# Attention and gated experts in one kernel: late attention steps between whole expert chunks, a reordered fifth pair, weight merges in two steps, two bank copies of seven on DVE

## The chip, the cores and the metric

The kernel runs on one core of one Trainium2 chip. The metric is the device time of one execution in microseconds; what is shown is the median of several runs. A profile is one further execution, with its own time.

## The reference

The program first does attention over 8 batches x 8 heads, 576 positions and 64 columns a head, with a mask by blocks of 64, and then passes the heads' outputs, 4608 tokens of 512 columns, through a two-layer feed-forward with a sigmoid gate.

```
scores = scale * np.matmul(q, k.transpose(0, 1, 3, 2))       # scale = 1/8
scores = np.where(block_i >= block_j, scores, -1e9)          # blocks of 64
attn = np.exp(scores - scores.max(-1, keepdims=True))
attn = attn / (attn.sum(-1, keepdims=True) + 1e-9)
x = np.matmul(attn, v).transpose(0, 2, 1, 3).reshape(B * S, H * D)
h = x @ w_in                                                 # 512 -> 2048
out = (h * (1 / (1 + np.exp(-1.702 * h)))) @ w_out           # 2048 -> 512
```

The weights arrive as 64-bit floats, and the kernel makes 32-bit floats of them itself.

## The kernel before, in words

**Attention.** Two heads make a pair; there are 32 pairs, four to a batch, and "the first pair" is pair 0. A pair's 576 queries go in five chunks, 0 to 4, of growing width (chunk i sees the keys up to its own blocks). `score` makes the scores of a list of chunks on TensorE (PE) into PSUM banks, DVE adds the mask and takes the row's extreme (`weigh`, L351), ACT takes the exponential (L358), DVE makes the reciprocal of the sum (L368, L371), and POOL, or DVE for chunk 4 of the late pairs, scales (`normalise`, L376, L378). The result must be transposed before the sum over the values. In the first eight pairs ("early") PE does it (`flip`, L102) and ACT copies the banks to SBUF (L411; the narrow tails L424). In the later pairs DVE transposes 32x32 blocks (`turn`, L385 the wide part, L390 the narrow one) and 16 DMAs move the blocks. `av` is the sum over the values on PE; ACT copies its bank to the ring `xr` (L450, L451). `prep` transposes the next pair's q and k on DVE (L297) and starts the load of the pair after.

**Order of the attention steps.** Three strings in `ORDER` give the steps of a pair in slots, one string for each phase (pairs 0 to 3, 4 to 7, 8 and later); `START` stands for pair 4 and `HANDOVER` for pair 8. Digits are chunks to score ("3+0/2+1": two banks for 3 and 0, two for 2 and 1), V is `av` of the pair before, L is `prep` of the next pair, a, B and C are flips (a: chunks 0 and 1 of this pair; B: 2 and 3 of the one before; C: 4 of the one before), and a dash is an empty slot. After each slot the main loop lets weights be converted up to a quota (`WEIGHTS_BY`: position, pieces; a pair is two positions) and experts run up to a quota (`TILES_BY`).

**Experts.** `moe` is a generator. Tokens go in 12 tiles of 384, the hidden columns in 16 chunks of 128. Numbers are split into a high and a low part (`split` for the tokens: xh on ACT, L498, xl on DVE, L82), and each product is three matmuls. A chunk is 12 matmuls into the bank `hp`, then ACT's tanh (L555), DVE's `g` (L556), ACT's `gh` (L564) and POOL's `gl` (L82); behind the 12 matmuls `second` issues the nine of the chunk before into three `acc` banks. There is one `hp` bank. The generator yields after every three matmuls, and `advance` stops there as soon as the quota is reached, so an attention step can stand within the 12 or within the nine.

**Weights.** There are 32 pieces of 128x512. `begin` has ACT scale the word that holds the exponent, to a PSUM bank (L219); `merge` puts the 32-bit word together on DVE in three steps (L223 shift, L229 sign, L234 low bits); `split_weights` makes the high part on ACT (L243) and the low part on POOL (L82). Each piece uses the same bank, and the merged word `z` stands in one of two rooms by turns for the first 28 pieces. The first tile's chunks call `convert` themselves for what they need.

Within an engine the instructions stand in one order; a scheduler makes it from the order of the code and from priorities (`tc.high_priority`), and PE's matmuls keep the order of the code.

Of the kernel before, what the change touches and what calls it, by code (L numbers as in the profile page):

```python
# [13 lines left out]
AF = mybir.ActivationFunctionType  # L14
ALU = mybir.AluOpType
# [10 lines left out]
ORDER = (  # L26
# [3 lines left out]
)  # L30

START = "1+0 - B 2/3 L C - V - 4 - a - - -"
HANDOVER = "B C - 3+0/2+1 - - V - - - 4 - - L - -"


WEIGHTS_BY = ((0, 0), (8, 13), (14.5, 32))
TILES_BY = ((8.4, 0), (17, 1), (33.7, 4), (65.7, -2))


# [1 line left out]
def attention_moe_kernel(  # L41
# [9 lines left out]
    nc = tc.nc  # L51
# [19 lines left out]
    def f(ap):  # L71
        return ap.bitcast(F32)
# [141 lines left out]

    def begin(j):

        bits[j] = ps.tile([P, 512], F32, tag="w3", name="wm")
        for w, c in parts[j]:
            nc.scalar.activation(out=bits[j][:, c], in_=f(w[..., 1]), func=AF.Copy, scale=2.0**-112)  # L219

    def merge(j):
        u = bits.pop(j).bitcast(U32)
        nc.vector.tensor_scalar(  # L223
            out=u, in0=u, scalar1=3, scalar2=None, op0=ALU.logical_shift_left
        )

        z = whole[j] = room("e1" if j % 2 and j < 2 * len(places) else "wm", [P, WC], U32, "wm")
        for w, c in parts[j]:
            nc.vector.scalar_tensor_tensor(  # L229
                out=u[:, c], in0=w[..., 1], scalar=0x80000000, in1=u[:, c],  # L230
                op0=ALU.bitwise_and, op1=ALU.bitwise_or,
            )
        for w, c in parts.pop(j):
            nc.vector.scalar_tensor_tensor(  # L234
                out=z[:, c], in0=w[..., 0], scalar=29, in1=u[:, c],
                op0=ALU.logical_shift_right, op1=ALU.bitwise_or,
            )

    def split_weights(j):
# [52 lines left out]
    def prep(n):  # L292

        tag = "e0" if early(n) and n % 2 else "qk"
        qk[n] = d2.tile([P, 2, S], F32, tag=tag, name="qk", bufs=1)
        for x in range(2):
            nc.vector.transpose(out=qk[n][:, x], in_=raw[n][:, x].rearrange("p c d -> p (c d)"))  # L297
        raw.pop(n)
        m = follower(n)
        if m is not None:  # L300
            load(m)
# [99 lines left out]
    def flip(n, chunks):  # L401

        for i in chunks:
            todo = [(j, hd) for j in range(i) for hd in range(2)]
            for x in range(0, len(todo), 4):
                part = todo[x : x + 4]
                bk = bank()
                for y, (j, hd) in enumerate(part):
                    tr(out=bk[:, y * P : (y + 1) * P], in_=es[i][:, hd, j * P : (j + 1) * P], identity=ident)
                s0 = SLOT[i] + part[0][0]  # L410
                nc.scalar.copy(  # L411
                    out=pw[:, :, s0 : s0 + len(part) // 2].rearrange("p b s h c -> p (s h) b c"),
                    in_=bk[:, 0 : len(part) * P].rearrange("p (x b c) -> p x b c", b=4, c=32),
                )

        bk = bank()
        todo = [(i, hd) for i in chunks for hd in range(2)]
        for y, (i, hd) in enumerate(todo):
            tr(out=bk[0:BLK, y * P : (y + 1) * P], in_=es[i][:, hd, i * P : width(i)], identity=ident)
        src = bk[0:BLK, 0 : len(todo) * P].rearrange("p (x b c) -> p x b c", b=4, c=32)  # L420
        for part in ([0], [1]) if 0 in chunks else (chunks,):
            i, x, a = part[0], 2 * chunks.index(part[0]), 2 if part[0] else 0
            s0 = 9 + max(i, 1)
            nc.scalar.copy(  # L424
                out=pw[0:BLK, a : a + 2, s0 : s0 + len(part)].rearrange("p b s h c -> p (s h) b c"),
                in_=src[:, x : x + 2 * len(part), a : a + 2],
            )
# [81 lines left out]
    def moe():  # L509
# [17 lines left out]
        for t in range(NT):  # L527
            tt = TILES[t][1]
            if t == 0:
                yield ("tile", 0)  # L530
                split(0)
            xh, xl = xs["xh"], xs["xl"]
            acc = [ps.tile([P, DM], F32, tag=f"acc{c}", name=f"acc{c}") for c in range(tt // P)]
            for fc in range(NFC):
                if t == 0:
                    convert(fc // FG * GROUP + NDC + fc % FG + 1)
                hp = ps.tile([P, 512], F32, tag="h", name="hp")
                fs = slice(fc % FG * P, (fc % FG + 1) * P)
# [12 lines left out]
                gh = d2.tile([P, TT], F32R, tag="gh", name="gh")[:, 0:tt]  # L551
                gl = d2.tile([P, TT], F32R, tag="gl", name="gl")[:, 0:tt]

                with tc.high_priority(offset=300):
                    nc.scalar.activation(out=g, in_=hp[:, 0:tt], func=AF.Tanh, scale=1.702)  # L555
                    nc.vector.scalar_tensor_tensor(  # L556
                        out=g, in0=g, scalar=1.0, in1=hp[:, 0:tt], op0=ALU.add, op1=ALU.mult
                    )

                if fc == NFC - 1 and t + 1 < NT:  # L560
                    yield ("tile", t + 1)
                    split(t + 1)
                with tc.high_priority(offset=300):
                    nc.scalar.copy(out=gh, in_=g)  # L564
                    subtract(nc.gpsimd, gl, g, f(gh))
                if prev is not None:
                    yield from second(prev)
                prev = (gh, gl, fc, acc, t)
        yield from second(prev)


# [7 lines left out]
        return -(-sum(TILES[t]) // S) * H  # L579

    mo = moe()
    state = {"t": 0.0, "wait": None, "done": False}

    def advance(heads_done, until):
        while not state["done"] and not until():
            if state["wait"] is not None:
                if heads_for(state["wait"]) > heads_done:
                    return
# [2 lines left out]
            if got is None:  # L591
                state["done"] = True
            elif isinstance(got, tuple):
                state["wait"] = got[1]
            else:
                state["t"] += got

    def before_av(n):
# [53 lines left out]
```

## Time and profile before

| | |
|---|---|
| median of 3 runs | 1127.14 us (1125.93 to 1127.29) |
| the profiled execution, its own time | 1124.21 us |
| its span, first to last instruction | 1122.4 us |
| mean granted TensorE clock | 0.989 |
| busy: PE, DVE, ACT, POOL | 1076.8, 585.3, 497.9, 407.2 us |
| read from and written to HBM | 45.09 and 9.44 MB |

The page has the engines' busy time, the same in 40 slices, and the costliest groups of instructions by line, with the idle time of the engine ahead of them and what ended it. A row of the timeline gives start, duration, engine, line, operation, out<-in and shapes, and in brackets the idle time ahead and its releaser. Consecutive matmuls overlap in these rows, so their pace is the distance of their starts.

### The profile page before, as it was taken

The page shows a single profiled execution, that of the slowest core. Times are in us where ns is not written, and L with a number is a line of the kernel's source. Part 1 is how long each engine was busy: PE and PEld are TensorE (multiplying, and loading weights), DVE is VectorE, ACT ScalarE, POOL GpSimd, SP SyncE. Part 2 cuts the span into 40 slices and gives each one's busy share as a digit, 9 for nine tenths or more (in the row PEclk, how much of TensorE's full clock was granted, in tenths as well). Part 3 has the DMA queues.
Part 4 walks back from the last instruction along what each step waited for, and adds up shares of the span by engine and source line. Part 5 has one row for each costly group of instructions (what it writes and reads, how often), then busy time and mean ns, then how long its engine had stood idle before and what let it go on. Part 6 is the DMA issues. An engine that isn't in the chain of part 4 may idle for free. (4 is left out here: it accounts for less than half of the span.)

```text
span 1122.4 us, 20015 instructions
## 1 busy us (share of the span) xinstructions
PE 1076.8 (96%) x6960; PEld 910.8 (81%) x6960; DVE 585.3 (52%) x1856; ACT 497.9 (44%) x1321; POOL 407.2 (36%) x509
## 2 busy tenths in 40 slices
PE   5979998999999999999999999999999999999998
PEld 3757776788788888888888888888888888999997
DVE  6785885555555645655545655654545655111210
ACT  5865776434434534433443543443434444322322
POOL 4665674333333333233333333333333233222222
PEclk8979999999999999999999999999999999999999
DMA  8734533233443433243443333244343331200000
GB/s 167 207 89 153 144 69 72 77 80 64 103 86 79 102 88 72 56 109 64 95 100 79 81 94 68 52 113 86 74 111 73 70 87 46 54 29 1 29 1 29
DMA packets 219366, 91.26 MB, mean 81 GB/s; under 512 B 197760, under 2 KB 197760, under 8 KB 219264
## 3 DMA queue, kind: packets, MB, share of 16 engines
q1 hardware_dynamic: 214528, 89.38, 33.9%
q8 instruction: 55, 0.90, 0.3%
q10 hardware_dynamic: 4736, 0.59, 0.3%
q14 instruction: 47, 0.39, 0.1%
HBM read 45.09 MB, written 9.44 MB: 49 GB/s over the span
## 5 line engine op out<-in xcount | busy, mean ns | idle before, releaser
L82 POOL TENSOR_TENSOR gl<-g,gh 128x384 fp32r<-128x384 f32 x192 | 194.8, 1015 | 538.8 <-ACT gh L564 448.1
L99 PE MATMUL hp<-xh,wih 128*128 128x384 f32 x768 | 265.2, 345 | 11.7 <-DVE g L556 10.9
L556 DVE SCALAR_TENSOR_TENSOR g<-g,hp 128x384 f32<-128x384 f32 x192 | 105.5, 550 | 326.4 <-ACT g L555 325.4
L99 PE MATMUL hp<-xh,wil 128*128 128x384 f32 x768 | 259.3, 338 | 0.1
L99 PE MATMUL hp<-xl,wih 128*128 128x384 f32 x768 | 254.5, 338 | 0.6 <-DVE xl L82 0.4
L555 ACT ACTIVATE g<-hp 128x384 f32<-128x384 f32 x192 | 94.1, 490 | 339.9 <-PE hp L99 337.7
L99 PE MATMUL acc<-woh,gh 128*128 128x512 f32 x576 | 232.1, 403 | 0.0
L99 PE MATMUL acc<-woh,gl 128*128 128x512 f32 x576 | 227.2, 394 | 0.5 <-POOL gl L82 0.5
L99 PE MATMUL acc<-wol,gh 128*128 128x512 f32 x576 | 227.6, 395 | 0.0
L99 PEld LDWEIGHTS hp<-xh,wih 128*128 128x128 f32 x768 | 144.5, 188 | 36.4 <-DVE g L556 21.8
L564 ACT CAST gh<-g 128x384 fp32r<-128x384 f32 x192 | 98.5, 513 | 147.9 <-DVE g L556 147.8
L358 ACT ACTIVATE e<-e,mx 64x64 f32<-64x64 f32 (+4 forms) x240 | 132.4, 552 | 63.6 <-DVE mx L351 63.6
L376 POOL TENSOR_TENSOR e<-e,sm 64x64 f32<-64x64 f32 (+1 forms) x192 | 114.1, 614 | 108.9 <-DVE sm L371 62.0
L99 PEld LDWEIGHTS hp<-xh,wil 128*128 128x128 f32 x768 | 144.7, 188 | 7.4 <-POOL wil L82 0.7
L99 PEld LDWEIGHTS hp<-xl,wih 128*128 128x128 f32 x768 | 144.1, 188 | 1.7 <-DVE xl L82 1.7
L99 PE MATMUL bank<-qk 64*128 64x320 f32 (+4 forms) x768 | 122.2, 428 | 14.2 <-DVE qk L297 11.1
L99 PEld LDWEIGHTS acc<-woh,gh 128*128 128x128 f32 x576 | 108.3, 188 | 30.6 <-issue 10.7
L99 PEld LDWEIGHTS acc<-wol,gh 128*128 128x128 f32 x576 | 108.1, 188 | 23.5 <-POOL wol L82 0.2
L99 PEld LDWEIGHTS acc<-woh,gl 128*128 128x128 f32 x576 | 108.3, 188 | 16.8 <-POOL gl L82 1.2
L385 DVE STREAM_TRANSPOSE turned<-e 128x384 f32<-128x384 f32 (+1 forms) x192 | 92.4, 499 | 48.2 <-POOL e L376 48.2
L99 PEld LDWEIGHTS bank<-qk 64*128 64x128 f32 x768 | 69.8, 194 | 56.5 <-issue 26.5
L351 DVE CUSTOM_DVE_ANT_0 e<-bank,mask 64x64 f32<-64x64 f32 (+4 forms) x240 | 88.3, 417 | 29.8 <-PE bank L99 26.4
(50 smaller groups left out, 960.5 us busy)
## 6 DMA issues: line engine op xcount, KB each, us to landing
turned<-turned SPq DMA_DIRECT2D x192, 80.0 KB, 2.1
turned<-turned SPq DMA_DIRECT2D x96, 112.0 KB, 2.2
raw<-in_q_dram SPq DMA_DIRECT2D x128, 72.0 KB, 2.5
out_dram<-osb SPq DMA_DIRECT2D x36, 256.0 KB, 2.2
raw<-in_k_dram SPq DMA_DIRECT2D x120, 72.0 KB, 2.5
turned<-turned SPq DMA_DIRECT2D x96, 88.0 KB, 2.1
words<-in_moe_w_in_dram SPq DMA_DIRECT2D x16, 512.0 KB, 6.1
vp<-in_v_dram SPq DMA_DIRECT2D x60, 128.0 KB, 2.3
```

Source lines behind the costliest of these rows:

```text
L82: eng.tensor_tensor(out=out, in0=in0, in1=in1, op=ALU.subtract)
L99: return tc.keep_in_program_order(nc.tensor.matmul(**kw))
L351: nc.vector.tensor_tensor_reduce(out=e[0:m, hd, lo:hi], in0=s, in1=mk, op0=ALU.add, op1=ALU.min, scale=-0.125, scalar=3e38 if lo == 0 else ...
L358: nc.scalar.activation(out=e[0:m, hd], in_=e[0:m, hd], func=AF.Exp, scale=-1.0, bias=mx[0:m, i, hd : hd + 1], accum_out=sm[0:m, i, hd : hd ...
L376: nc.gpsimd.tensor_tensor(out=x, in0=x, in1=sc.to_broadcast([m, width(i)]), op=ALU.mult)
L385: nc.vector.transpose(out=tw[:, :, SLOT[i] : SLOT[i] + i, hd].rearrange("p b j c -> p j b c"), in_=e[:, hd, 0 : i * P],)
L555: nc.scalar.activation(out=g, in_=hp[:, 0:tt], func=AF.Tanh, scale=1.702)
L556: nc.vector.scalar_tensor_tensor(out=g, in0=g, scalar=1.0, in1=hp[:, 0:tt], op0=ALU.add, op1=ALU.mult)
L564: nc.scalar.copy(out=gh, in_=g)
```

## The change

1. `advance` goes on, from pair 9 on, until the generator stands at an "edge": behind the nine matmuls of a chunk and ahead of the next chunk's 12. In those pairs an attention step no longer stands within a chunk.
2. In the late pairs' string and at the hand-over V stands one slot earlier or nearer the scores; at the hand-over C stands one slot later.
3. `START`: in the fifth pair B comes first, and C and V of the fourth pair stand ahead of the fifth's scores 2 and 3.
4. The merge has two DVE steps: first z = low word >> 29, then z = (bank << 3) | z. The sign now comes with ACT's pass, which is Prelu with a slope of -2^32 where it was Copy.
5. Of a pair's seven wide bank copies in `flip`, DVE takes two: the first bank of chunk 3 and the first of chunk 4.
6. `WEIGHTS_BY` asks for 11 pieces by position 6.5, none more until 8.9, and all 32 by 14.5.
7. The transposes of `prep` get a higher priority up to pair 4.

```
-    "3+0/2+1 - - - - V - 4 - - - L -",
+    "3+0/2+1 - - - V - - 4 - - - L -",
-START = "1+0 - B 2/3 L C - V - 4 - a - - -"
-HANDOVER = "B C - 3+0/2+1 - - V - - - 4 - - L - -"
-WEIGHTS_BY = ((0, 0), (8, 13), (14.5, 32))
+START = "B 1+0 C V - L 2/3 - - 4 - a - -"
+HANDOVER = "B - C - 3+0/2+1 - - V - - 4 - - L - -"
+WEIGHTS_BY = ((0, 0), (6.5, 11), (8.9, 11), (14.5, 32))
...
-            nc.scalar.activation(out=bits[j][:, c], in_=f(w[..., 1]), func=AF.Copy, scale=2.0**-112)
+            nc.scalar.activation(
+                out=bits[j][:, c], in_=f(w[..., 1]), func=AF.Prelu, scale=2.0**-112, alpha=-(2.0**32)
+            )
...
-        nc.vector.tensor_scalar(
-            out=u, in0=u, scalar1=3, scalar2=None, op0=ALU.logical_shift_left
-        )
-        for w, c in parts[j]:
+        for w, c in parts.pop(j):
+            nc.vector.tensor_scalar(
+                out=z[:, c], in0=w[..., 0], scalar1=29, scalar2=None, op0=ALU.logical_shift_right
+            )
             nc.vector.scalar_tensor_tensor(
-                out=u[:, c], in0=w[..., 1], scalar=0x80000000, in1=u[:, c],
-                op0=ALU.bitwise_and, op1=ALU.bitwise_or,
-            )
-        for w, c in parts.pop(j):
-            nc.vector.scalar_tensor_tensor(
-                out=z[:, c], in0=w[..., 0], scalar=29, in1=u[:, c],
-                op0=ALU.logical_shift_right, op1=ALU.bitwise_or,
+                out=z[:, c], in0=u[:, c], scalar=3, in1=z[:, c],
+                op0=ALU.logical_shift_left, op1=ALU.bitwise_or,
             )
...
+        with tc.high_priority(offset=300 if n <= HP else 0):
+            for x in range(2):
+                nc.vector.transpose(out=qk[n][:, x], in_=raw[n][:, x].rearrange("p c d -> p (c d)"))
...
-                nc.scalar.copy(
+                (nc.vector.tensor_copy if i > 2 and x == 0 else nc.scalar.copy)(
...
                 prev = (gh, gl, fc, acc, t)
+                yield ("edge", fc)
...
-        while not state["done"] and not until():
+        while not state["done"] and not (until() and (state["edge"] or turns["n"] <= 2 * HP)):
...
             elif isinstance(got, tuple):
-                state["wait"] = got[1]
+                if got[0] == "tile":
+                    state["wait"] = got[1]
+                else:
+                    state["edge"] = True
             else:
+                state["edge"] = False
                 state["t"] += got
```

How this moves instructions is seen in the order in which each engine's instructions stand. PE, at the first group of scores of a late pair; bank<-qk are scores, hp and acc are the experts. Before:

```order
L99 MATMUL hp<-xh,wil 128x384
L99 MATMUL hp<-xl,wih 128x384
L99 MATMUL bank<-qk 128x448 x2
L99 MATMUL bank<-qk 128x64 x2
L99 MATMUL bank<-qk 128x320 x2
L99 MATMUL bank<-qk 128x192 x2
L99 MATMUL acc_5869<-woh,gh 128x512
L99 MATMUL acc_5869<-woh,gl 128x512
```

and now:

```order
L99 MATMUL acc_5839<-woh,gl 128x512
L99 MATMUL acc_5839<-wol,gh 128x512
L99 MATMUL bank<-qk 128x448 x2
L99 MATMUL bank<-qk 128x64 x2
L99 MATMUL bank<-qk 128x320 x2
L99 MATMUL bank<-qk 128x192 x2
L99 MATMUL hp<-xh,wih 128x384
L99 MATMUL hp<-xh,wil 128x384
```

The scores stood between a chunk's 12 and the nine of the one before; now they stand ahead of a chunk's 12.

DVE, from the first scores of a late pair on, in the changed program; it reads alike in many pairs before, and in other pairs of both the first g stands ahead of the second narrow transpose (L389 here, L390 before; L384 is the wide one, g<-g,hp is the step that frees hp):

```order
L367 TENSOR_SCALAR sm<-sm 64x2
L370 RECIPROCAL sm<-sm 64x2
L389 STREAM_TRANSPOSE turned<-e 64x2x2x32
L367 TENSOR_SCALAR sm<-sm 128x2
L370 RECIPROCAL sm<-sm 128x2
L389 STREAM_TRANSPOSE turned<-e 64x2x2x32
L556 SCALAR_TENSOR_TENSOR g<-g,hp 128x384 x2
L384 STREAM_TRANSPOSE turned<-e 128x3x4x32 x2
```

DVE did not move here, but the first g now belongs to the chunk right behind the scores.

DVE, behind the scores of chunk 4 of a late pair. Before:

```order
L368 TENSOR_SCALAR sm<-sm 128x2
L371 RECIPROCAL sm<-sm 128x2
L378 TENSOR_SCALAR e<-e,sm 128x576 x2
L385 STREAM_TRANSPOSE turned<-e 128x4x4x32 x2
L556 SCALAR_TENSOR_TENSOR g<-g,hp 128x384
L390 STREAM_TRANSPOSE turned<-e 64x2x2x32
```

and now:

```order
L367 TENSOR_SCALAR sm<-sm 128x2
L370 RECIPROCAL sm<-sm 128x2
L377 TENSOR_SCALAR e<-e,sm 128x576 x2
L556 SCALAR_TENSOR_TENSOR g<-g,hp 128x384
L384 STREAM_TRANSPOSE turned<-e 128x4x4x32 x2
L389 STREAM_TRANSPOSE turned<-e 64x2x2x32
```

The g moved ahead of the two wide transposes; in some pairs it stands between the two scalings.

ACT, up to the copy of the fourth pair's V (xr<-bank 128x512). Before:

```order
L243 CAST woh<-wm 128x512
L219 ACTIVATE wm<-words 128x512
L358 ACTIVATE turned,sm<-turned,mx 128x320 x2
L358 ACTIVATE turned,sm<-turned,mx 128x448 x2
L411 COPY turned<-bank 128x4x4x32
L243 CAST wih<-wm 128x512
L219 ACTIVATE wm<-words 128x512
L411 COPY turned<-bank 128x4x4x32
L424 COPY turned<-bank 64x2x2x32
L451 COPY xr<-bank 128x512
```

and now:

```order
L241 CAST wih<-wm 128x512
L220 ACTIVATE wm<-words 128x512
L411 COPY turned<-bank 128x4x4x32
L424 COPY turned<-bank 64x2x2x32
L241 CAST wih<-wm 128x512
L220 ACTIVATE wm<-words 128x512
L450 COPY xr<-bank 128x64
L451 COPY xr<-bank 128x512
```

The exponentials of the fifth pair's chunks 2 and 3 (320 and 448 wide) left the stretch, and one wide bank copy went to DVE.

More of the change, by code (lines that the diff above doesn't have):

```diff
@@ L295, in prep @@
         qk[n] = d2.tile([P, 2, S], F32, tag=tag, name="qk", bufs=1)
-        for x in range(2):
-            nc.vector.transpose(out=qk[n][:, x], in_=raw[n][:, x].rearrange("p c d -> p (c d)"))
+        with tc.high_priority(offset=300 if n <= HP else 0):
+            for x in range(2):
+                nc.vector.transpose(out=qk[n][:, x], in_=raw[n][:, x].rearrange("p c d -> p (c d)"))
         raw.pop(n)
@@ L581, in attention_moe_kernel @@
     mo = moe()
-    state = {"t": 0.0, "wait": None, "done": False}
+    state = {"t": 0.0, "wait": None, "done": False, "edge": True}
     def advance(heads_done, until):
-        while not state["done"] and not until():
+        while not state["done"] and not (until() and (state["edge"] or turns["n"] <= 2 * HP)):
             if state["wait"] is not None:
```

## The prediction

> **What bounds the kernel now.** I read the page first, then the busy time by stretches, then the waits and the timeline at the places that the change touches. The page:
>
> ```profile
> span 1122.4 us, 20015 instructions
> PE 1076.8 (96%) x6960; PEld 910.8 (81%) x6960; DVE 585.3 (52%) x1856; ACT 497.9 (44%) x1321; POOL 407.2 (36%) x509
> PEclk8979999999999999999999999999999999999999
> ```
>
> TensorE is busy for 96% of the span, so only time in which it waits can be won. The stretches (span, then busy time of PE, PEld, DVE, ACT, POOL, granted clock) say where it waits:
>
> ```profile
> 0.00:90.00 90.00, 67.37 (x515) 49.79 (x516) 66.15 (x217) 60.16 (x176) 51.22 (x74) 0.87 0.60 144
> 90.00:215.00 125.00, 115.12 (x793) 92.44 (x793) 87.06 (x252) 82.59 (x216) 69.11 (x76) 1.00 0.40 107
> 215.00:985.00 770.00, 760.84 (x4992) 648.58 (x4991) 412.44 (x1354) 316.87 (x854) 254.38 (x327) 1.00 0.36 81
> 985.00:1110.00 125.00, 125.00 (x629) 113.37 (x628) 18.52 (x34) 34.59 (x70) 30.51 (x30) 1.00 0.04 13
> ```
>
> PE idles 22.6 us in the first 90, 9.9 in the next 125, 9.2 in the 770 of the late pairs, and nothing in the pure expert stretch. The change works on the first three. What the last one shows is the floor of a chunk, from the chain of waits:
>
> ```profile
> 1003.03 2.10 PE hp L99 x12
> 1005.14 2.08 PE acc L99 x9
> ```
>
> A chunk costs 4.18 us, and everything below is measured against it.
>
> **Late pairs: the wait that goes, and the one that comes.** The waits between 230 and 985 us have one line for PE's long waits, and the timeline shows one of them (PE, then DVE):
>
> ```profile
> PE hp L99 <- DVE g L556: 9.2, 21, 1.6
> ...
> 629.56 0.40 PE L99 MATMUL acc<-wol,gh 128*128 128x512 f32 x1
> 630.19 0.44 PE L99 MATMUL hp<-xh,wih 128*128 128x384 f32 x1 [0.23 <-DVE g L556]
> 630.47 0.34 PE L99 MATMUL hp<-xh,wil 128*128 128x384 f32 x1
> ...
> 627.53 0.95 DVE L378 TENSOR_SCALAR e<-e,sm 128x576 f32<-128x576 f32 x2
> 628.40 1.30 DVE L385 STREAM_TRANSPOSE turned<-e 128x512 f32<-128x512 f32 x2
> 629.62 0.51 DVE L556 SCALAR_TENSOR_TENSOR g<-g,hp 128x384 f32<-128x384 f32 x1
> ```
>
> There is one bank for hp, so a chunk can't begin before DVE has read the last one's hp in g (L556); here g stands behind two scalings and two transposes of chunk 4. The start distance is 0.63 instead of 2.08/9 = 0.23, so 0.40 are lost, of which the view counts 0.23 as idle; the matmul behind it follows after 0.28 instead of 2.10/12 = 0.175, another 0.11. So the 21 waits cost 9.2 + 21 x (0.17 + 0.11) = 15.1 us.
>
> With the change DVE's order puts g ahead of the two transposes (1.30 us). But attention now stands directly ahead of an hp, so a new wait is possible at two places. The rows for both (PE, DVE of the first group 3+0/2+1; PE, DVE of chunk 4):
>
> ```profile
> 604.37 2.11 PE L99 MATMUL bank<-qk 64*128 64x448 f32 x16
> 606.41 0.50 PE L99 MATMUL acc<-woh,gh 128*128 128x512 f32 x1
> ...
> 610.54 0.31 DVE L390 STREAM_TRANSPOSE turned<-e 64x128 f32<-64x128 f32 x1 [1.66 <-POOL e L376]
> ...
> 622.94 1.24 PE L99 MATMUL bank<-qk 64*128 64x256 f32 x8
> 624.11 0.49 PE L99 MATMUL acc<-woh,gh 128*128 128x512 f32 x1
> ...
> 623.66 0.55 DVE L556 SCALAR_TENSOR_TENSOR g<-g,hp 128x384 f32<-128x384 f32 x1
> 624.13 0.42 DVE L351 CUSTOM_DVE_ANT_0 e<-bank,mask 128x256 f32<-128x256 f32 x1
> ```
>
> *Behind 3+0/2+1.* The scores begin at U = 604.37; the next matmul is 2.04 later. In the new order that is hp, then acc, and the second hp is due at 2.04 + 0.11 + 2.10 + 2.08 = U + 6.33. Where DVE's g stands behind the last narrow transpose of chunk 3, which waits for POOL until U + 6.17, g ends at 6.17 + 0.31 + 0.55 = U + 7.03: 0.7 to 0.8 late, with the restart 0.9. Counted in the changed order, 12 of the 23 late pairs have it so; in the others g stands ahead of that transpose, or V stands between and pushes the hp back. 12 x 0.9 = 10.8 us.
>
> *Behind chunk 4.* Scores at T = 622.94, hp at T + 1.17, the second hp due at 1.17 + 0.11 + 4.18 = T + 5.46. DVE's scalings end at 628.48 = T + 5.54, after a reduction that began at T + 1.19 only because g (623.66) was ahead of it; the new g is done before. If the chain starts up to 0.46 sooner, g ends near T + 5.6, otherwise T + 6.05. That is 0.15 to 0.6 late; I take the near end, 0.3 with the restart, since that g is no longer in front. In 14 pairs g stands behind both scalings: 4.2 us. In the others it stands between them and is in time. Two pairs have the next tile's split ahead of this g; I give them a wait like today's, 0.5 each: 1.0.
>
> Sum: 10.8 + 4.2 + 1.0 = 16.0 against 15.1: **1 us lost**, so the late part nearly cancels. Bounds: 11 us won (the first wait absent), 10 lost (it stands in all 23 pairs: 11 more x 0.9). Behind a waiting hp stand the rest of its chunk and all later work of PE, so each wait counts in full. V one slot earlier costs nothing: it comes at least four chunks (17 us) after the scores of chunk 4, and the transposes that it needs end at 629.70, T + 6.8. The quotas still give six chunks a pair, and each interruption costs PE its two switches as before.
>
> **Start: to the first expert chunk.** ACT copies, DVE merges, the weights' ping-pong and V of the fourth pair (ACT; then PE; then groups):
>
> ```profile
> 58.13 0.62 ACT L243 CAST woh<-wm 128x512 fp32r<-128x512 f32 x1 [1.81 <-DVE wm L234]
> 61.57 0.62 ACT L243 CAST woh<-wm 128x512 fp32r<-128x512 f32 x1 [2.29 <-DVE wm L234]
> 65.00 0.62 ACT L243 CAST woh<-wm 128x512 fp32r<-128x512 f32 x1 [0.98 <-DVE wm L234]
> 70.50 0.57 ACT L358 ACTIVATE turned<-turned,mx 128x320 f32<-128x320 f32 x1
> ...
> 72.24 0.67 ACT L358 ACTIVATE turned<-turned,mx 128x448 f32<-128x448 f32 x1
> ...
> 75.96 0.58 ACT L451 COPY xr<-bank 128x512 f32<-128x512 f32 x1 [0.74 <-PE bank L99]
> ...
> 34.74 1.98 PE L99 MATMUL bank<-qk 64*128 64x320 f32 x8
> ...
> 76.71 0.44 PE L99 MATMUL hp<-xh,wih 128*128 128x384 f32 x1 [0.71 <-ACT xr L450]
> ...
> 81.83 0.45 PE L99 MATMUL hp<-xh,wih 128*128 128x384 f32 x1 [1.79 <-DVE g L556]
> ...
> L223 DVE TENSOR_SCALAR wm<-wm 128x512 uint32<-128x512 uint32 x32 | 22.3, 696 | 16.0 <-ACT wm L219 15.9
> L411 ACT COPY turned<-bank 128x512 f32<-128x512 f32 x32 | 17.4, 582 | 5.2 <-PE bank L102 5.0
> L82 POOL TENSOR_TENSOR wil<-wm,wih 128x512 fp32r<-128x512 f32 x16 | 20.5, 1280 | 14.1 <-ACT wih L243 13.0 <-PE hp L99 1.1
> ```
>
> A piece of weights turns over in 61.57 - 58.13 = 3.44 us, with ACT waiting for three DVE steps of 0.70. Two steps remain, and the first no longer needs ACT, so one step lies between ACT's two: about 1.4 less a piece. Of the 1.81 + 2.29 + 0.98 = 5.1 us of ACT idle, 1.5 stay: 3.6 won. Four bank copies of 0.58 leave ACT's queue in these two pairs: 2.3. The exponentials of the fifth pair's 2 and 3 (70.50 to 72.91) move behind V: 2.4. Two more pieces are converted ahead of V, as WEIGHTS_BY now asks: two ACT steps of 0.62 each, 2.5 lost. Their loads move ahead with them on SP's queue, two pieces before they are used: nothing. The four copies of the first two pairs give at most 2.3, half taken: 1.2. So V's copy at 75.96 comes 3.6 + 2.3 + 2.4 - 2.5 + 1.2 = 7.0 earlier; PE still has to do the moved scores (1.98): **5 us won** (0 to 8). Prelu for Copy is the same kind of ACT pass, and the new program has one table load as before: nothing. The fifth pair's transposes with a higher priority stand ahead of merges that they stood among: nothing, since V is not behind them. The first chunk then waits from 76.71 to 81.83 for 2.1 us of work; g is behind a conversion that is behind four xl on DVE. Three of them now stand ahead: **1 won** (0 to 2).
>
> The new first step reads SBUF and writes SBUF; no row has it. DVE and POOL side by side are seen in xl:
>
> ```profile
> 76.05 3.50 DVE L82 TENSOR_TENSOR xl<-xr,xh 128x384 fp32r<-128x384 f32 x4
> ...
> 192.41 1.51 DVE L82 TENSOR_TENSOR xl<-xr,xh 128x384 fp32r<-128x384 f32 x3 [7.24 <-ACT xh L498]
> ```
>
> 0.87 each while POOL works, 0.50 while it idles. So I take the new step no cheaper than the 0.70 of a removed one; 0.87 / 0.50 times that is its upper end, 0.5 us a piece, 1.5 over three. The Trainium skill (VectorE: DVE Perf Modes, "The perf-mode tier table") gives a 32-bit single-source step within SBUF twice the speed; by that it takes an estimated 0.35 and the sum would be 1 us better. The same skill (GPSIMD Engine Reference, the row "SBUF interfaces") has DVE instructions in such modes, or with two SBUF inputs, contend with GpSimd, and the two rows of xl agree.
>
> The clock was 0.87 over these 90 us; PE's matmuls at half clock are part of the losses. The Trainium skill (TensorE: Matmul & The Clock Gate, Part 1) ties half clock to an idle window of about 3.4 us; by it a start that idles 7 us less gets back an estimated 0.13 x 7 = 0.9 us more.
>
> **Fifth to eighth pair.** Over eight pairs DVE loses 32 steps of 0.70 (22 us) and gains 16 copies at 0.58 to 0.70, ACT's price and its own for 512 columns from a bank (9 to 11 us). Most of that lies beside PE's work; the hp waits for g that it can shorten are few: **1 won** (2 lost to 3 won). At the hand-over:
>
> ```profile
> 187.83 0.33 PE L102 MATMUL bank<-ident,turned 128*128 128x128 f32 x1 [1.07 <-POOL turned L376]
> 190.16 1.20 PE L102 MATMUL bank<-ident,turned 128*128 128x128 f32 x9 [2.00 <-POOL turned L376]
> ```
>
> PE waits 3.07 us for the normalised chunk 4, which stood behind the last merges on DVE. In the new order these merges end before that chunk's scores, and C comes one slot later: **2.5 won** (0 to 3). V now follows the scores at once, on the same three banks; the three hp that stood between them (0.5 us) no longer cover its wait, which is in the bound.
>
> **The rivals.** *The late wait moves only in part* (no new wait behind 3+0): the late part wins 11, total 1127.14 - 9.5 - 11 = 1106.6. For it: the hp wait has slack wherever g is early; against: the order. *The start's saving is eaten by POOL*, whose seven subtractions of 1.28 in the stretch up to V (9 us, beside its normalising) fill what ACT frees. The new first step writes z, so it waits for the subtraction two pieces back, and with it DVE's queue, the reductions and g: start 0 to 1 won, total about 1124. *The conversions come late*, the one that ends slower: 21 pieces now lie between positions 8.9 and 14.5, where the expert chunks 4, 8 and 12 need their weights. A wait decides once a chunk's weights are more than two pieces behind; at 2 us a piece, three such waits of 4 us make 12: about 1131. Against it: four pairs take the 125 us of the second stretch, so 2.8 pairs leave 87 us for 21 pieces, 4.1 each. *The new wait is in all late pairs*: 10 more, about 1128.5. That the edits do not take effect is excluded by the order itself.
>
> **How the numbers follow.** 5 + 1 + 1 + 2.5 - 1 = 8.5 us. From the profiled 1124.2 (span 1122.4 and 1.8 around it) that gives 1115.7; the runs' median is 2.9 above it, so 1127.14 - 8.5 = 1118.6, said as 1119. Chances: forecast 0.47, first rival 0.15, POOL 0.16, late conversions 0.12, all late pairs 0.10. About 0.2%, 2.25 us, is what a measurement can tell: faster means below 1124.9, slower above 1129.4. The forecast and the first rival are faster, as is half of the POOL case: 0.70. The rest of that case and most of the last are the same: 0.15. Late conversions and the last one's upper end: 0.15. Range 1108 to 1129: the forecast's own bounds are 1113 to 1125; it leaves out half of the first rival and the late conversions.
>
> **What would show it.** Right: V's copy of the fourth pair before 71, ACT's wait for wm under 1.5 us a piece, no POOL wait at the hand-over over 1 us, and PE's waits for g at U + 6.3 in about half of the late pairs, some 0.8 each. Wrong: first hp still after 75, hp waiting for wih, wil or woh, or PE's waits for g in 215 to 985 adding to under 4 or over 15 us of idle.

## The result and the profile after

The changed kernel takes 1136.44 us (median of 4 runs, 1135.55 to 1137.16), the kernel before 1127.11 (4 runs, 1125.93 to 1127.29) beside it. The ratio is 1.0085 (95% interval 1.0067 to 1.0102): about 9.6 us slower, where 8.5 us were forecast as won. The profiled execution takes 1135.84 us with a span of 1133.9. The spans differ by 11.5 us, not by 9.6, since the profiled execution of the kernel before, 1124.21 us, lies 2.9 below its median.

The page of the changed kernel:

```profile
span 1133.9 us, 19957 instructions
PE 1080.7 (95%) x6960; PEld 910.1 (80%) x6960; DVE 569.5 (50%) x1840; ACT 494.4 (44%) x1305; POOL 408.1 (36%) x509
```

The work left DVE and ACT as intended: DVE is busy 569.5 us instead of 585.3, ACT 494.4 instead of 497.9. TensorE has the same 6960 matmuls and a longer span. The same stretches as before say where:

```profile
0.00:90.00 90.00, 67.67 (x520) 49.95 (x521) 61.49 (x216) 56.90 (x170) 52.37 (x75) 0.89 0.56 133
90.00:215.00 125.00, 111.92 (x769) 89.97 (x769) 71.78 (x223) 76.19 (x201) 69.31 (x76) 0.97 0.41 114
215.00:985.00 770.00, 756.17 (x4952) 639.72 (x4950) 413.29 (x1361) 317.88 (x849) 251.87 (x325) 1.00 0.36 81
985.00:1110.00 125.00, 125.00 (x630) 113.34 (x629) 20.76 (x38) 37.19 (x76) 29.51 (x29) 1.00 0.04 13
```

The first 90 us are slightly better. The next 125 hold 769 matmuls instead of 793, at a clock of 0.97. The late pairs have 13.8 us of idle TensorE instead of 9.2. The same places of TensorE's program, in us from the start of the span:

| place | before | after | difference |
|---|---|---|---|
| first hp | 76.7 | 73.1 | -3.6 |
| V of the fifth pair | 113.8 | 111.5 | -2.3 |
| V of the sixth | 143.4 | 149.0 | +5.7 |
| V of the seventh | 171.1 | 177.1 | +6.0 |
| V of the eighth | 196.9 | 200.5 | +3.6 |
| chunk 16's hp | 203.7 | 208.1 | +4.4 |
| chunk 160's hp | 981.9 | 993.4 | +11.5 |

So 3.6 us are won up to the first hp and 1.3 lost again behind it, 8.0 are lost between two neighbouring V, 2.4 are won at the hand-over, of which 0.8 go again, and 7.1 are lost over the late pairs.

**The late pairs.** The line of the waits between 230 and 985 us (us in total, times, longest):

```profile
PE hp L99 <- DVE g L556: 13.8, 17, 1.5
```

The timeline at one wait behind 3+0/2+1 (PE, then DVE, then POOL; start, duration):

```profile
613.07 2.11 PE L99 MATMUL bank<-qk 64*128 64x448 f32 x16
...
619.17 0.40 PE L99 MATMUL acc<-wol,gh 128*128 128x512 f32 x1
620.25 0.44 PE L99 MATMUL hp<-xh,wih 128*128 128x384 f32 x1 [0.68 <-DVE g L556]
...
619.30 0.31 DVE L389 STREAM_TRANSPOSE turned<-e 64x128 f32<-64x128 f32 x1 [2.00 <-DMA raw<-in_q_dram]
619.64 0.56 DVE L556 SCALAR_TENSOR_TENSOR g<-g,hp 128x384 f32<-128x384 f32 x1
...
617.43 1.83 POOL L375 TENSOR_TENSOR e<-e,sm 128x448 f32<-128x448 f32 x2 [0.73 <-DVE sm L370]
```

With U = 613.07 the transpose starts at U + 6.23, behind POOL's scaling, which ends at 619.26 (the view names a DMA as the last releaser, but POOL's end fits). The g ends at U + 7.13 and hp starts at U + 7.18 instead of U + 6.33. The start distance behind the last acc is 1.08, so 0.85 are lost, and 0.11 more in the restart.

Counted by start distances, a wait is what the first hp of a chunk starts later behind the last acc than the 0.23 us of a free succession. Between 225 and 990 us there are 31 such waits, 18.7 us, in three sorts. Twelve are as above, 0.85 each. Fourteen stand behind chunk 4, 0.15 each, too short for the view of waits. Five are larger, 6.5 us together: three where a tile ends (1.65, 1.16, 0.49) and two one chunk behind a V that stands directly ahead of an hp (1.61 each). One at a tile's end, DVE then PE:

```profile
292.96 3.44 DVE L82 TENSOR_TENSOR xl<-xr,xh 128x384 fp32r<-128x384 f32 x4
296.32 0.54 DVE L556 SCALAR_TENSOR_TENSOR g<-g,hp 128x384 f32<-128x384 f32 x1
...
296.92 0.45 PE L99 MATMUL hp<-xh,wih 128*128 128x384 f32 x1 [1.48 <-DVE g L556]
```

The split's four xl (3.44 us) stand ahead of g, and the next tile's first hp waits. Before, the same count gives 23 waits of 12.9 us. With 0.11 for each restart that is 22.1 us against 15.4: 6.7 of the 7.1.

**The sixth pair.** TensorE's waits between 110 and 150 us, of the kernel before:

```profile
PE bank L102 <- ACT turned L411: 1.6, 1, 1.6
PE bank L99 <- DVE mx L351: 0.2, 1, 0.2
```

Of the changed kernel:

```profile
PE hp L99 <- ACT wih L241: 3.3, 1, 3.3
PE bank L102 <- ACT xr L451: 1.5, 1, 1.5
PE bank L99 <- DVE mx L350: 1.3, 1, 1.3
PE hp L99 <- POOL wil L82: 0.7, 1, 0.7
```

The window from 135 to 145 us, of before and then of after (the granted clock is the third number from the right):

```profile
135.00:145.00 10.00, 10.00 (x80) 8.27 (x80) 8.50 (x21) 7.61 (x19) 4.99 (x5) 1.00 0.48 114
```

```profile
135.00:145.00 10.00, 6.29 (x23) 5.16 (x24) 7.08 (x14) 7.30 (x17) 6.54 (x7) 0.66 0.58 111
```

1.8 us of waits became 6.8, and after the longest one (chunk 8 waits for its weights) the clock is 0.66 for 10 us, worth another (1 - 0.66) x 10 = 3.4. That makes 5.0 + 3.4 = 8.4 against the 8.0 of the table.

### The profile page after: what moved, and what is told of

It reads as the page before. It is cut to its first block, busy times and chain, and to the rows that moved or that the text cites. A ratio compares the mean times of both kernels' runs of the same rounds, so it can differ in the third digit from the quotient of the medians.

```text
span 1133.9 us, 19957 instructions
## 1 busy us (share of the span) xinstructions
PE 1080.7 (95%) x6960; PEld 910.1 (80%) x6960; DVE 569.5 (50%) x1840; ACT 494.4 (44%) x1305; POOL 408.1 (36%) x509
## 5 line engine op out<-in xcount | busy, mean ns | idle before, releaser
L99 PE MATMUL hp<-xh,wih 128*128 128x384 f32 x768 | 272.3, 355 | 18.4 <-DVE g L556 15.0
L99 PE MATMUL acc<-woh,gh 128*128 128x512 f32 x576 | 225.8, 392 | 0.0
L99 PE MATMUL bank<-qk 64*128 64x320 f32 (+4 forms) x768 | 121.9, 427 | 12.8 <-DVE qk L296 8.9
L99 PEld LDWEIGHTS acc<-woh,gl 128*128 128x128 f32 x576 | 108.2, 188 | 18.7 <-POOL gl L82 0.9
L384 DVE STREAM_TRANSPOSE turned<-e 128x384 f32<-128x384 f32 (+1 forms) x192 | 92.3, 499 | 49.6 <-POOL e L375 48.8
```

Source lines behind the costliest of these rows:

```text
L99: return tc.keep_in_program_order(nc.tensor.matmul(**kw))
L384: nc.vector.transpose(out=tw[:, :, SLOT[i] : SLOT[i] + i, hd].rearrange("p b j c -> p j b c"), in_=e[:, hd, 0 : i * P],)
```

## The experiments

All times are medians; "by the ratio" is the ratio to the runs of before on the same chip, less 1, times 1125 us. Its interval is about 1.5 us to either side, about 1 for e5, e7, e12, e13, e14 and e17.

### The late pairs: two edits, each alone and together

e4 puts the late part alone into the kernel before, e1 takes it out of the changed kernel, e9 keeps the rule only ahead of chunk 4:

```
e4: before, with the lines on "edge" and
+    "3+0/2+1 - - - V - - 4 - - - L -",
e1: after, with
-        while not state["done"] and not (until() and (state["edge"] or turns["n"] <= 2 * HP)):
+        while not state["done"] and not until():
+    "3+0/2+1 - - - - V - 4 - - - L -",
e9: before, with the lines on "edge" and
+        while not state["done"] and not (until() and (state["edge"] or not edge)):
...
+            advance(heads_done, lambda: state["t"] >= lim, n >= 2 * HP and order(n)[sl + 1 : sl + 2] == ["4"])
```

e4: 

> The kernel before with the rule on chunk edges and the earlier V in the late pairs, nothing else. Theory: the late waits go from 15 to 22 us, so 1127.1 + 7 = 1134 us. Rival (the late loss comes only from where the early changes put the tiles' ends among the pairs): 1127, within 1.5 us.

e1: 

> Theory (two separate losses: TensorE's waits for g in the late pairs cost 22 us instead of 15, and the conversions that stand still between positions 6.5 and 8.9 make chunk 8 wait for its weights): with the rule on chunk edges and V's slot in the late pairs as in the kernel before, the late waits go back to about 15 us, so 1136.4 - 7 = 1129.5 us, and the wait of 3.3 us for wih near 138 us stays. Rival (the late waits are only where an early delay is paid, so that the late part is neutral): 1136, within 1 us.

e9: 

> The kernel before with the rule on chunk edges only ahead of the scores of chunk 4, not ahead of those of 3+0/2+1; V and everything early as before. Theory (the two edges are two terms: behind chunk 4 the wait falls from 0.61 + 0.11 to 0.15 + 0.11 in most pairs, behind 3+0/2+1 a new wait of 0.85 + 0.11 comes in 12 pairs): only the first term stays, so the late waits fall from 15 to 4 or 5 us and the kernel takes 1127 - 10 = 1117 us. Rival (the loss is in any interruption at a chunk's edge, since TensorE then needs both the new hp and DVE at once): 1130 or more.

Measured: e4 1133.37 us (ratio 1.0070, 1.0055 to 1.0085), 7.9 slower than before. e1 1129.55 (1.0039, 1.0025 to 1.0053): less than the changed kernel by 6.9 us by the medians and 5.2 by the ratios, and 4.4 more than before. The traces separate it better: from chunk 16's hp to chunk 160's the changed kernel takes 7.1 us more than before, e4 7.3 and e1 0.0, and e4 has as many waits as the changed kernel (31, 18.7 us). So the late part costs some 7 us whatever stands early, and the early part 4.4. e9 1119.85 (0.9957, 0.9944 to 0.9969): 4.8 us faster than before, the fastest kernel here. In it the line of the same waits is:

```profile
PE hp L99 <- DVE g L556: 4.0, 5, 1.5
```

By start distances e9 has 22 waits of 7.3 us: sixteen of 0.15 behind chunk 4 and the three at tiles' ends (1.65, 1.16, 1.18) carry most. The expected 10 us were too many because the last three were not among the terms that go.

The two edits of the late part, apart:

```
e17: before, with
-    "3+0/2+1 - - - - V - 4 - - - L -",
+    "3+0/2+1 - - - V - - 4 - - - L -",
e18: e4 without that line
e15: after, with the condition of e9
```

e17: 

> The kernel before with V of the late pairs one slot earlier, nothing else. Theory (the late loss is the rule ahead of the scores of 3+0/2+1; V's slot is nothing by itself): 1125 to 1127 us, no difference. Rival (V's slot is a loss too, as the changed kernel with the rule only at chunk 4 suggests, which got 5 us slower, not 12 faster, with waits of 3.8 us where a tile's split stands right at V): 1130 us or more, and such waits in it.

e18: 

> The kernel before with the rule on chunk edges ahead of both groups of scores, V's slot as before. With the early V it was 1133.4 us, with the rule only at chunk 4 and the old V 1119.9. Theory (the rule ahead of 3+0/2+1 is the loss): 1132 to 1134 us, 12 waits for g of 0.85 us. Rival (the early V is the loss): 1120 to 1122 us.

e15: 

> The changed kernel with its rule on chunk edges only ahead of the scores of chunk 4. If the late part is a term by itself, the 12 us between the two forms of the rule are won here too (before with the rule 1133.4, with the rule only at chunk 4 1119.9): 1136.4 - 12 = 1124.5 us. Rival (the early V slot or the place of the tiles' ends keeps a part of the loss): 1128 or more.

Measured, as us slower than before by the ratio; "stage" is the same from chunk 16's hp to chunk 160's in the trace, and "half clock" what a granted clock of 0.50 took from TensorE there (half of the time for which it lasted):

| | V as before | V one slot earlier |
|---|---|---|
| no rule | 0 | e17 +3.4 (1.0030, 1.0019 to 1.0041); stage +3.1, half clock 3.4 |
| rule ahead of 4 only | e9 -4.8; stage -4.9, half clock 0 | e15 +16.0 (1.0142, 1.0128 to 1.0157), with the early part; stage +10.9, half clock 5.1 |
| rule ahead of both | e18 +10.6 (1.0094, 1.0079 to 1.0109); stage +10.5, half clock 1.7 | e4 +7.9; stage +7.3, half clock 0 |

The rule ahead of 3+0/2+1 is the loss: e18 against e9, 15.4 us with V as it was. e18 has the twelve waits, eleven of 0.85 and one of 0.92, 11.6 us with their restarts. Most of the rest is one more wait of 2.90 and the half clock behind it, from 440.3 to 443.6: 4.6.

My theory falls for V, whose slot costs 3.4 by itself. It is not that the waits add up to more: e17 has 15 of them, 12.8 us, where the kernel before has 23 of 12.9. They are fewer and longer, and behind two of them, 2.21 and 2.22 us in the view, the clock is 0.50 for 3.4 us each time. A further 1.0 us of e17 lies ahead of chunk 16, where its edit changes nothing. One of the two stretches:

```profile
559.60:563.00 3.40, 3.40 (x12) 3.40 (x13) 0.91 (x3) 0.33 (x1) 1.00 (x1) 0.50 0.00 0
```

The 2.7 us between e18 and e4 do not show that the early V saves anything beside the full rule: they are no more than e18's wait of 2.90 with its half clock, and 1.2 us that e18 had lost ahead of chunk 16, where its edit changes nothing. Where the rule stands only at chunk 4, the early V makes the kernel worse: 16.0 - 4.4 = 11.6 for the late part of e15, of which 5.1 are half clock behind waits of 1.78, 3.65 and 3.66 us. One of the two longest (PE, ACT, DVE):

```profile
556.82 2.98 PE L99 MATMUL bank<-turned,vp 128*64 128x128 f32 x60
566.79 0.44 PE L99 MATMUL hp<-xh,wih 128*128 128x384 f32 x1 [3.65 <-DVE g L556]
...
561.28 0.56 ACT L451 COPY xr<-bank 128x512 f32<-128x512 f32 x1
561.85 0.93 ACT L498 CAST xh<-xr 128x384 fp32r<-128x384 f32 x2
...
565.24 1.02 DVE L82 TENSOR_TENSOR xl<-xr,xh 128x384 fp32r<-128x384 f32 x2
566.19 0.55 DVE L556 SCALAR_TENSOR_TENSOR g<-g,hp 128x384 f32<-128x384 f32 x1
```

A tile's split stands right at V: it needs V's copies, which stand on ACT behind the new exponentials; the xl stand on DVE behind the transposes of 2+1, and g stands behind the xl.

### The early pairs: one edit at a time

```
e5: before, with the new begin and merge (Prelu, two steps)
e6: before, with
+                (nc.vector.tensor_copy if i > 2 and x == 0 else nc.scalar.copy)(
e7: before, with the new START, HANDOVER and the priority in prep
e14: e5 and e7 together
e8: e1, with
+                nc.scalar.copy(
e2: after, and e3: e1, with
+WEIGHTS_BY = ((0, 0), (8, 13), (14.5, 32))
```

e5: 

> The kernel before with the two-step merge and Prelu, nothing else. Theory (the loss between 113 and 135 us comes from the order of the early pairs, START and HANDOVER: ACT's copies of the turned banks now stand behind exponentials and conversions): the shorter merge only wins, 2 to 4 us at the start: 1124 us. Rival (the merge itself is what makes the early part later, because its first step must wait for POOL to let the word buffer go): 1129 to 1132 us.

e6: 

> The kernel before with two of seven bank copies on DVE, nothing else. Theory: 16 copies leave ACT, of which the start shows 1 to 2 us: 1126 us, within 1. Rival (the copies on DVE stand behind merges and g, and TensorE waits for the banks): 1129 or more.

e7: 

> The kernel before with the new START, HANDOVER and the priority of the early transposes, nothing else. Theory (the order carries the early loss): 1130 to 1132 us, with the loss between 113 and 137 us and TensorE waiting for ACT's bank copies. Rival: the hand-over's 2.4 us are won and no more: 1124.5.

e14: 

> The kernel before with the two-step merge and the new START, HANDOVER and transposes' priority, nothing else. Alone the one made no difference, the other cost 1.2 us. If the early edits simply add: 1126.5 us. If merge and order hurt each other (with the new conversion dates on top, and no copies on DVE, the kernel was 6 us slower than before): 1130 or more.

e8: 

> The changed kernel with the late part of before and all bank copies on ACT again: against the run with the late part undone (1129.6) it shows what the copies on DVE do beside the other early edits. Theory (order): 1130.5, the start 1 us later. Rival (copies cost): 1127 or less.

e2: 

> Theory: with the conversions' dates of the kernel before, the wait of hp for wih near 138 us (about 6 us with its half clock) goes: 1136.4 - 6 = 1130.5 us; up to 2 us of it may come back at the start, where two pieces less are converted. Rival (the two-step merge, which now writes and reads the word buffer that POOL also reads, is the cost of the early part, whatever the dates): still within 1.5 us of 1136.

e3: 

> Theory: both losses go and what was won at the start (3.6 us) and at the hand-over (2.4 us) stays: 1136.4 - 13 = 1123.5 us, 3 to 4 us under the kernel before. Rival (merge and copies on DVE cost by themselves): not under 1127.

Measured against before, with what it does to two stages of TensorE's program:

| kernel | us, ratio (interval) | by the ratio | first hp | V of fifth to V of sixth |
|---|---|---|---|---|
| e5 merge | 1125.79, 1.0001 (0.9992 to 1.0010) | +0.1 | +2.2 | +4.3 |
| e6 copies | 1129.76, 1.0036 (1.0022 to 1.0050) | +4.1 | +1.9 | +1.0 |
| e7 orders | 1127.18, 1.0011 (1.0002 to 1.0020) | +1.2 | -2.6 | -0.1 |
| e14 merge, orders | 1127.58, 1.0017 (1.0008 to 1.0025) | +1.9 | -1.4 | +5.2 |
| e8 merge, orders, dates | 1131.18, 1.0051 (1.0039 to 1.0064) | +5.7 | -1.7 | +8.6 |
| e3 merge, orders, copies | 1131.54, 1.0055 (1.0039 to 1.0070) | +6.2 | -4.5 | +5.0 |
| e1 all four | 1129.55, 1.0039 (1.0025 to 1.0053) | +4.4 | -3.1 | +7.9 |
| e2 after, old dates | 1138.11, 1.0113 (1.0096 to 1.0130) | +12.7 | -3.0 | +5.2 |

Two theories fall. The dates are not the cause: with the old ones the wait for wih is gone and some 3 us less are lost between the two V, and still the kernel is 1.8 (e3 against e1) to 3.1 us (e2 against after) slower; in both traces the time is lost again around the hand-over, where the clock is 0.50 twice, for 3.4 us each. Nor are the orders, which alone or with the merge cost under 2. Every kernel of the table with the new merge loses 4 to 5 us between the two V, and the new dates bring it to 8. Part of this is half clock: 1.7 us in e5, e2 and e3, 3.4 in e14, e1 and the changed kernel, 5.1 in e8. TensorE's waits from 110 to 150 us, of the merge alone (e5) and then the largest two of e3:

```profile
PE bank L99 <- DVE mx L349: 3.0, 1, 3.0
PE bank L102 <- ACT turned L409: 0.9, 1, 0.9
```

```profile
PE bank L102 <- ACT turned L411: 2.9, 1, 2.9
PE bank L99 <- ACT turned L411: 1.0, 1, 1.0
```

The window in which the clock fell, of e5 and then of e3:

```profile
125.00:135.00 10.00, 8.62 (x43) 7.03 (x44) 6.74 (x28) 6.99 (x20) 6.42 (x8) 0.83 0.38 154
```

```profile
125.00:135.00 10.00, 6.72 (x39) 5.55 (x39) 9.10 (x28) 7.42 (x22) 6.73 (x7) 0.91 0.46 176
```

The wait has another name in each kernel, but both have one of about 3 us, and matmuls at half clock after it, as the changed kernel has. The merge alone gets its loss back at the hand-over (V of the seventh to V of the eighth: 2.6 won, without the new HANDOVER) and so shows nothing in the total. The copies alone lose 1.7 us from V of the sixth to V of the seventh, where TensorE waits 2.3 us instead of 0.5, and 2.9 from there to V of the eighth. In this second stretch TensorE waits 4.1 us as it does before; what differs is the clock, of e6 and then of before:

```profile
192.70:199.50 6.80, 5.74 (x20) 4.97 (x22) 2.23 (x4) 2.28 (x5) 1.01 (x1) 0.50 0.00 0
```

```profile
190.00:197.00 7.00, 6.34 (x39) 4.64 (x41) 3.60 (x16) 4.74 (x14) 0.64 (x3) 1.00 0.00 1
```

The edits don't add: the copies cost 4.1 alone and 4.3 beside merge and orders, but win 1.3 where the new dates stand too (e8 to e1).

### What makes the sixth pair late

```
e12: e5, and e10: e1, with a third buffer for the merged words:
+            d2.tile([P, WC], U32, tag="osb", name="wm", bufs=3) if j % 3 == 2 and j < 2 * len(places)
+            else room("e1" if j % 3 and j < 2 * len(places) else "wm", [P, WC], U32, "wm")
e11: e1, with the first merge step written back into the words:
+                out=w[..., 0], in0=w[..., 0], scalar1=29, scalar2=None, op0=ALU.logical_shift_right
e13: e5, and e16: e1, with
+        with tc.high_priority(offset=300 if early(n) else 0):
             nc.vector.tensor_tensor_reduce(
```

e12: 

> The kernel before with the two-step merge, nothing else, and one more buffer for the merged words. The merge alone gave no difference from before. Theory (its saving is eaten by the waits for POOL): with them gone the saving shows, 1123 to 1124 us, and TensorE's wait of 3.0 us for DVE's reductions near 125 us goes. Rival: no difference from before again, 1125.5 to 1127.

e10: 

> The changed kernel with the late part of before (1129.6 us) and one more buffer for the merged words, in a tag that is idle until piece 28. Theory (the two-step merge writes that buffer in its first step, so DVE's queue waits for POOL's subtraction two pieces back, 10.0 us in 9 waits against 0.5 before, with reductions and g behind it): these waits fall under 4 us and the kernel takes 1126 us, 3 to 4 less. Rival (the early loss is the order of the pairs and the weights' dates; the waits for POOL lie beside other waits): 1129, within 1.

e11: 

> The changed kernel with the late part of before (1129.6 us), the first merge step written back into the word buffer instead of the merged one: only the second step then waits for POOL, later by one step and the wait for ACT. Theory: part of the gain of one more buffer, 1127.5 to 1129, if the strided write costs no more than 0.3 us a piece (0.43 us now). Rival (no wait for POOL is behind the loss): 1130 to 1131 by the slower write.

e13: 

> The kernel before with the two-step merge, nothing else, and DVE's mask reductions of the eight early pairs with a higher priority, so that in the sixth pair one merge step instead of two, and none between, stands ahead of the reductions of chunk 4. The merge alone lost 4.3 us between V of the fourth and of the fifth pair. Theory (what eats the merge's saving is DVE's order there: TensorE's fourth bank waits 3.0 us for reductions behind merges and g): that wait falls to about 1.5 us or less, the matmuls behind it keep their full clock, and the kernel takes 1122 to 1123.5 us. Rival (the wait only changes its place, since ACT and POOL are late too): 1125 to 1127, no difference from the merge alone.

e16: 

> The changed kernel with the late part of before (1129.6 us) and the reductions' priority. Theory as for the merge with the priority: 1126 to 1127.5. Rival (in the changed kernel the wait for the weights at chunk 8, 3.3 us, is what counts, and it doesn't depend on DVE's order there): 1129 to 1130.

Measured: e12 1125.60 (1.0004, 0.9993 to 1.0014), e10 1130.04 (1.0051, 1.0037 to 1.0064), e11 1128.78 (1.0037, 1.0024 to 1.0049): none differs from the kernel that it was made from. DVE's waits for POOL between 45 and 205 us fell from 10.0 to 6.7 in e10 and to 4.3 in e11, less than I had wanted in e10, since the last pieces still share one buffer. In e12 the 3.0 us wait for the reductions stayed. So the waits for POOL are real, but lie beside other waits.

e13 1126.17 (1.0009, 0.9997 to 1.0021): the wait for the reductions fell from 3.0 to 1.7, and the clock fell all the same, so the stage from V of the fifth to V of the sixth (named one pair too low in what was expected) still loses 4.4. e16 1135.43 (1.0085, 1.0072 to 1.0098): 5 us worse than e1, with a wait of 3.6 us for ACT's xr at the hand-over, where e1 has 1.65. DVE's place of the reductions is therefore not the cause by itself. What is shown is that the new merge makes this pair late: the traces of all 13 kernels that have it lose 4.3 us or more between the two V, those of the six other changed ones 1.0 at most. Which edge of the chain ACT, DVE, POOL does it stays open. A likely reading, not shown, is that conversions now fill queues that the old ones left free when a score or a copy came.

## Why the prediction was wrong

The forecast was 8.5 us won; in the traces 11.5 are lost. Of these 20.0 us of error the fifth to the eighth pair have 9.3, the late pairs 6.1, the first chunk 2.3, the start 1.4 and the hand-over 0.9.

**Late pairs: one term mis-sized.** Behind 3+0/2+1 the count (12), the due time (U + 6.33) and the lateness were right: 0.85 + 0.11 measured, 0.9 said. Behind chunk 4 fourteen waits of 0.15 + 0.11 against 0.3 said. The step that failed is "Two pairs have the next tile's split ahead of this g; I give them a wait like today's, 0.5 each: 1.0": five waits, 6.5 + 5 x 0.11 = 7.1 us. Of these, two belong to "V stands between and pushes the hp back": it does, but the g behind the transposes of 2+1 comes 1.6 later still. So the term is +7, not +1.

**"V one slot earlier costs nothing" failed too**: +3.4 alone, by e17. I had looked at what V waits for, not at the split that waits for V and stands ahead of g; by e17's trace the price is the half clock behind two such waits, not their sum.

**Start.** 5 said, 3.6 won at the first hp; V's copy stands at 73.3, not before 71. The turn of a piece is right: casts at 60.44, 62.34, 64.68, about 2 us, and waits of 0.76 for wm after a first one of 2.48. What remained is a long wait of TensorE ahead of it (PE, ACT, DVE):

```profile
64.16 0.63 PE L102 MATMUL bank<-ident,turned 128*64 128x128 f32 x4 [4.49 <-ACT xr L451]
...
60.44 0.62 ACT L241 CAST woh<-wm 128x512 fp32r<-128x512 f32 x1 [2.48 <-DVE wm L232]
...
58.02 0.78 DVE L296 STREAM_TRANSPOSE qk<-raw 128x576 f32<-128x576 f32 x1
58.72 0.89 DVE L229 TENSOR_SCALAR wm<-words 128x512 uint32<-128x512 uint32 x1
```

The cast stands on ACT ahead of V's copies of the third pair, the merge on DVE behind the transposes that got the priority, for which I had charged "nothing, since V is not behind them". TensorE's bank is.

**First chunk.** 1 said, nothing won: its waits are 0.89 and 1.44 beyond a free succession, against 2.05, and up to V of the fifth pair 1.3 us are lost.

**Fifth to eighth pair: the step that failed.** "Most of that lies beside PE's work; the hp waits for g that it can shorten are few: 1 won (2 lost to 3 won)" became 8.0 lost in the sixth pair alone, and 0.3 behind it. I looked for hp that wait for g. The waits there are for a bank copy, a reduction and the weights, each at an engine whose work shrank, and the half clock that follows a long one was in no term. The rival of late conversions named chunk 8, beside 4 and 12, and the size of a wait (4 us: 3.3 + 0.7); its cause is not the dates alone, since the old dates put other waits there.

**Hand-over.** 2.5 said, 2.4 won up to V; TensorE's wait inside V, with the scores right ahead of it, grew from 1.52 to 2.32 us, and 0.8 is given back by chunk 16.

**The new step on DVE** was taken at 0.70; it takes 0.41 to 0.43 undisturbed and 0.60 on average. The two steps in the view of groups (busy, mean ns):

```profile
L229 DVE TENSOR_SCALAR wm<-words 128x512 uint32<-128x512 uint32 x28 | 16.7, 597 | 5.4 <-POOL wol L82 3.3 <-POOL wil L82 1.4
L232 DVE SCALAR_TENSOR_TENSOR wm<-wm 128x512 uint32<-128x512 uint32 x28 | 19.2, 686 | 8.1 <-ACT wm L220 7.8
```

One of the shortest in the timeline:

```profile
122.91 0.41 DVE L229 TENSOR_SCALAR wm<-words 128x512 uint32<-128x512 uint32 x1
```

The half price that the Trainium skill gives (VectorE: DVE Perf Modes, "The perf-mode tier table") was nearer than mine for 20 of the 28 steps. The other 8 began while POOL was at work (see the end).

## What to carry over

To move an interruption to the boundary of a unit is only a gain if the work that the interruption starts is done before the unit's next hand-over: the same rule won 4.8 us ahead of the scores whose work leaves DVE in time and lost 15.4 ahead of the scores that wait for POOL. Where three engines pass work in order, an edit that frees one of them is worth what the next wait on the bounding engine allows, so each edit is measured alone, and in the stage that it touches: the merge won at one place what it lost at another. Whatever a moved step is waited for by counts as much as what it waits for.

## What was unexpected in the hardware

The clock fell after shorter waits than I had counted with. In the merge with priority a single wait of 1.68 us was followed by 0.50 from 124 to 130 us, in the pair orders of e7 one of 2.38 by 0.54 from 192 to 194. In the kernel before, waits of 1.60 near 130 us and of 1.07 and 2.00 close together at the hand-over left it at 1.00. The same two waits at the hand-over, 1.08 and 2.00 in e17 and 1.03 and 1.99 in e6, were followed by 0.50, for 3.4 and 6.8 us. What decides between the two, no run here shows. The wait in e13's timeline, and its windows:

```profile
124.41 1.43 PE L99 MATMUL bank<-qk 64*128 64x320 f32 x2 [1.68 <-DVE mx L350]
```

```profile
124.00:126.00 2.00, 1.59 (x3) 0.73 (x4) 1.29 (x8) 1.95 (x4) 2.00 (x3) 0.50 0.99 313
126.00:128.00 2.00, 2.00 (x6) 1.71 (x7) 1.96 (x7) 1.19 (x4) 0.29 (x1) 0.50 1.02 416
128.00:130.00 2.00, 2.00 (x9) 1.56 (x9) 0.00 (x0) 0.91 (x2) 1.86 (x2) 0.50 0.57 231
```

The Trainium skill (TensorE: Matmul & The Clock Gate, Part 1) ties half clock to an idle window of about 3.4 us. Here 1.7 us was enough once and 2.0 not another time, so a wait of that length is a risk of 1.7 or 3.4 us more, not a sum. A difference of that size between two kernels is read beside the clock before it is put down to an edit.

And a DVE step within SBUF that takes 0.41 to 0.43 us took up to 1.49 in the changed kernel. In the timeline of the merge alone (e5):

```profile
123.83 1.21 DVE L229 TENSOR_SCALAR wm<-words 128x512 uint32<-128x512 uint32 x1
...
123.76 1.00 POOL L82 TENSOR_TENSOR gl<-g,gh 128x384 fp32r<-128x384 f32 x1
124.71 1.45 POOL L82 TENSOR_TENSOR wil<-wm,wih 128x512 fp32r<-128x512 f32 x1
```

The step begins just behind POOL's gl and ends at 125.04, 0.28 after it; the subtraction that begins in the step takes 1.45 us, where 1.27 is usual. It is so throughout: of the 28 steps of the changed kernel, 8 begin while a POOL instruction has 0.29 us or more to go. They take 0.58 to 1.49 and end 0.28 or 0.29 us after that instruction. The other 20 take 0.41 to 0.43, also where POOL begins during the step, as in the one at 122.91 that is shown above. Then it is POOL's gl that takes longer, 1.18 us where 1.01 is the mean:

```profile
123.00 1.18 POOL L82 TENSOR_TENSOR gl<-g,gh 128x384 fp32r<-128x384 f32 x1 [0.30 <-POOL wil L82]
```

So here the two do not share their time: the one that begins second waits, and what the step costs depends on which of the two that is.
